# Retention attention and a Mish layer on one core: order of the first two token groups changed

## The chip, the core and the metric

The kernel runs on one core of a Trainium2 chip. A core has five engines that run their own instruction lists and wait for each other by semaphores: TensorE (PE in the profile, with its weight loads as PEld), VectorE (DVE), ScalarE (ACT), GpSimd (POOL) and SyncE (SP). Transfers between the chip's memory and the core's SBUF are issued by GpSimd, SyncE or ScalarE and carried out by 16 DMA engines. TensorE writes only into PSUM, eight banks, from which VectorE and ScalarE read.

The metric is the time of one execution on the device in microseconds (us), as a median of several runs. "Faster" means that this time falls.

## The reference

Two steps follow one another. The first is an attention without softmax, in which an earlier token counts the less the further back it is (factor `lam` per step, one `lam` per head), computed in blocks with a state that is carried on. The second is a layer of two matrix products with Mish between them. The shapes: 4 sequences (batches) of 768 tokens, 8 heads of 64; `w_in` is 512 x 2048, `w_out` 2048 x 512; all inputs and the output are float32.

```python
for b in range(nb):                       # blocks of 64 tokens
    sl = slice(b * block, (b + 1) * block)
    qb, kb, vb = (q[:, :, sl].copy(), k[:, :, sl].copy(), v[:, :, sl].copy())
    intra = np.einsum('bhic,bhjc->bhij', qb, kb) * Dmask[None]
    intra = np.einsum('bhij,bhjd->bhid', intra, vb)
    inter = np.einsum('bhid,bhde->bhie', qb * lam_pow[None], kv_state)
    out[:, :, sl] = intra + inter
    kb_dec = kb * rev_pow[None]
    kv_state = lam_block[None, :, None, None] * kv_state + np.einsum('bhsd,bhse->bhde', kb_dec, vb)
...
h = x @ w_in                              # x: attention output, 3072 tokens x 512
sp = np.where(h > 20.0, h, np.log1p(np.exp(np.minimum(h, 20.0))))
g = h * np.tanh(sp)
return (g @ w_out).astype(np.float32)
```

## The kernel before

The kernel takes blocks of 128 tokens instead of 64. A group n is one such block of all four batches, so 512 tokens; there are six groups, n = 0 to 5. For a group and a batch b the steps are these:

- **Turning k and q.** `turn_pe` transposes k and q of (n, b) on TensorE, four 128 x 128 pieces each, into a PSUM bank (L230), and a copy brings them to SBUF as `kT` and `qT`: by ScalarE (L238), or by VectorE where `by_vector` is set (L236). Later groups use `turn_dma` on SyncE's queue instead.
- **Scores.** `scores` makes eight products of 64 rows into two banks, e and o unless named otherwise (L256), and VectorE multiplies both with the decay mask into `sb` (L260).
- **Outputs.** In group 0 `first_outputs` multiplies `sb` with v so that x comes out transposed (L268), and ScalarE copies it to `xt` (L270). From group 1 on `outputs` adds the part of the state (L276) and of `sb` and v (L281) in one bank, VectorE scales it to `xn` (L284), and the transposition to `xt` is done by DMA or, with `turn` given, by a step `later` on TensorE (L293) and ScalarE (L295).
- **State.** `decay_k` scales k into `kd` (L249, VectorE or GpSimd), `state` multiplies it with v (L302); in group 0 VectorE makes the state `w` from it (L307), later VectorE adds the old state into `raw` (L310) and VectorE or GpSimd scales that to the new `w` (L312).

The first layer works on units of 128 columns of `w_in`. `unit` multiplies one such unit with all 512 tokens (L329) and ScalarE applies Mish (L335); `unit_part` does it for a range of tokens; `two_units` does two units for one half of the tokens (L355, L358). Its banks A, B and C go round. `dense2_plain` is one quarter of the second layer for one batch (L574). From the third group on, parts of both layers are computed with fewer products by sums (`x_sums`, `w_sum`, `token_sum`, `weight_sum`), which the change doesn't touch.

Nothing is scheduled automatically: the order of the calls is the order on each engine's list, and an engine takes its list strictly in that order. Buffers come from named places (`bufs` copies of each), and every PSUM bank is one place, so a step that reuses a bank waits until the last reader of the bank is done. `fill(m)` issues m products of zeros of 128 columns, `busy(m)` such of 512 columns; they keep TensorE busy.

All loads that also convert to 16 bits are issued by GpSimd in one queue (L82, L87, L96, L101). At the start it holds, in order, k and q of batch 1, v of batches 0 and 1, k and q of batches 2 and 3, v of batches 2 and 3, then `win0` in three pieces, `win2`, `win1`, and k, q, v of group 1 with `win3` between them. k and q of batch 0 come by SyncE's and ScalarE's queues.

In group 0 the order is: turn and score batch 0, turn batch 1, outputs of batch 0, scores of batch 1, and so on; `sb` has four places, of which two are used for each batch, so the scores of batch 2 wait for the outputs of batch 0. In group 1 each batch's outputs and state follow soon behind its scores, and the two upper batches are turned with the first lower outputs:

```python
    decay = out1(1)
    turn1(2, "eo")
    decay()
    decay_k(1, 2, nc.vector)
    later[1]()
    turn1(3)
    two_units(1, 0, 0)
    scores(1, 2)
```

Here `out1(b)` issues outputs and state of group 1, and `decay()` is the multiplication of L312 for a lower batch, on VectorE.

Of the kernel before, what the change touches and what calls it, by code (L numbers as in the profile page):

```python
# [8 lines left out]
F16 = mybir.dt.float16  # L9
AF = mybir.ActivationFunctionType  # L10
# [10 lines left out]
def kernel(  # L21
# [98 lines left out]
    load_first("q", 1)  # L120
    load_first("v", 0, 2)
    load_first("k", 2)
    load_first("q", 2)
# [4 lines left out]
    load_first("k", 3)  # L128
    load_first("q", 3)
# [121 lines left out]
    def scores(n, b, tags="eo"):  # L251
# [6 lines left out]
        for t in range(2):  # L258
            sb[n, b, t] = work.tile([128, JP, C], F16, name="sb", tag="sb", bufs=4)
            nc.vector.tensor_tensor(out=sb[n, b, t], in0=p_[t], in1=dm[:, t], op=ALU.mult)  # L260
# [11 lines left out]
    def outputs(n, b, turn=None):  # L272

        po = bank("z", [H, D])
# [361 lines left out]
    turn_pe(0, 1, first_banks, "k")  # L636
    turn_pe(0, 1, first_banks, "q", True)
    head_decays()
    fill(4)
    first_outputs(0, "C")  # L640
    fill(1)
    scores(0, 1, "AB")
    turn_pe(0, 2, first_banks)
    turn_pe(0, 3, first_banks, "k")
    fill(3)
    scores(0, 2)
    turn_pe(0, 3, first_banks, "q")
    first_outputs(1, "C")
    fill(3)
    scores(0, 3, "AB")  # L650
    nc.scalar.preload_act_table(AF.Mish)
    fill(2)
    first_outputs(2, "C")
    fill(4)
    unit_part(0, 0, "G", 0, 2 * C, True)
    first_outputs(3, "z")
    decay_k(0, 0, nc.vector)
    decay_k(0, 1, nc.vector)
    state_decays()
    decay_k(0, 2, nc.vector)  # L660
    decay_k(0, 3, nc.vector)
    unit_part(0, 1, "H", 0, 2 * C, True)
# [6 lines left out]
    unit(0, 3, "B")  # L669

# [10 lines left out]
    turn1 = lambda b, banks="Hz": turn_pe(1, b, banks)  # L681
# [3 lines left out]
    def out1(b):  # L685
        later[b] = outputs(1, b, "G")
        return state(1, b, "H", nc.vector if b < 2 else nc.gpsimd, b < 2)

    state(0, 2, "e", nc.vector)
    state(0, 3, "o", nc.vector)  # L690
# [9 lines left out]
    turn1(0)  # L700
    decay_k(1, 0, nc.vector)
    first_units(7)
# [4 lines left out]
    decay = out1(0)  # L707
    scores(1, 1)
    decay()
    first_units(14)  # L710
    later[0]()
    first_units(15)
    decay = out1(1)
    turn1(2, "eo")
    decay()
    decay_k(1, 2, nc.vector)
    later[1]()
    turn1(3)
# [14 lines left out]
    two_units(1, 10, 0)  # L733
# [5 lines left out]
    later[3]()  # L739
# [343 lines left out]
```

## Time and profile before

| | us |
|---|---|
| median of 3 runs | 206.59 (206.22 to 207.9) |
| profiled execution | 206.84 |
| its span, first to last instruction | 205.1 |
| TensorE busy | 194.9 (95% of the span) |
| VectorE busy | 146.3 (71%) |
| ScalarE busy | 99.8 (49%) |
| GpSimd busy, with its DMA issues | 81.3 (40%) |
| mean granted TensorE clock | 0.99 of full speed |

A row in order of time reads: start, duration, engine, line, operation, output <- input, shape, number, and in brackets how long the engine was idle just before and what ended that. A row of a transfer in the list of issues gives its size and the time from its issue to its landing. Products on TensorE are pipelined: the listed duration overlaps with the next, so the cost of a step is read from where it starts to where the next one starts. A row of a stretch gives its bounds, its length, the busy time of PE, PEld, DVE, ACT and POOL in it, the granted clock, the DMA share and GB/s.

### The profile page before, as it was taken

The page shows a single profiled execution, that of the slowest core. Times are in us where ns is not written, and L with a number is a line of the kernel's source. Part 1 is how long each engine was busy: PE and PEld are TensorE (multiplying, and loading weights), DVE is VectorE, ACT ScalarE, POOL GpSimd, SP SyncE. Part 2 cuts the span into 40 slices and gives each one's busy share as a digit, 9 for nine tenths or more (in the row PEclk, how much of TensorE's full clock was granted, in tenths as well). Part 3 has the DMA queues.
Part 4 walks back from the last instruction along what each step waited for, and adds up shares of the span by engine and source line. Part 5 has one row for each costly group of instructions (what it writes and reads, how often), then busy time and mean ns, then how long its engine had stood idle before and what let it go on. Part 6 is the DMA issues. An engine that isn't in the chain of part 4 may idle for free.

```text
span 205.1 us, 4646 instructions
## 1 busy us (share of the span) xinstructions
PE 194.9 (95%) x1918; PEld 149.9 (73%) x1918; DVE 146.3 (71%) x244; ACT 99.8 (49%) x179; POOL 81.3 (40%) x78
## 2 busy tenths in 40 slices
PE   7699999899999999999998999999999999999990
PEld 3577456688855566667767888888988988888890
DVE  6659628888987977689847698799588667179051
ACT  4566586748431224342263653555474484826300
POOL 7998453551292590848492369230000000000020
PEclk9979999999999999999999999999999999999999
DMA  9999999999989999999999989994112211002133
GB/s 130 139 168 206 174 168 157 173 207 187 122 145 175 202 143 163 166 114 106 140 201 232 120 66 140 187 197 110 29 26 80 76 56 51 0 3 104 50 105 104
DMA packets 109336, 26.26 MB, mean 128 GB/s; under 512 B 99458, under 2 KB 108802, under 8 KB 109314
## 3 DMA queue, kind: packets, MB, share of 16 engines
q0 software_dynamic: 77568, 13.37, 86.0%
q1 hardware_dynamic: 30704, 12.33, 29.2%
q10 hardware_dynamic: 1042, 0.26, 0.6%
q8 instruction: 15, 0.25, 0.5%
q14 instruction: 7, 0.06, 0.1%
HBM read 27.26 MB, written 6.29 MB: 164 GB/s over the span
## 4 chain that ended last, share of the span: by engine, by line
PE 77%; DMA 7%; DVE 6%; ACT 4%; issue 2%; POOL 1%; POOLq 0%; ACTq 0%; DVEq 0%
PE bG L523 13%; PE bH L523 12%; PE bB L412 5%; PE bC L412 4%; PE bA L329 4%; PE bC L329 3%; PE bA L412 3%; DMA xt<-xn 3%; DMA vz<-in_v_dram 3%; PE bB L329 3%; PE bC L355 3%; PE be L256 3%; PE bz L281 2%; PE bB L355 2%; PE bz L276 2%
## 5 line engine op out<-in xcount | busy, mean ns | idle before, releaser
L312 POOL TENSOR_TENSOR w<-raw,lbm 128x512 f16<-128x512 f32 x14 | 20.0, 1431 | 45.0 <-DVE raw L310 45.0
L523 PEld LDWEIGHTS <-gsum 128*128 128x128 f16 x336 | 31.2, 98 | 4.3
L523 PEld LDWEIGHTS <-hsg 128*128 128x128 f16 x240 | 23.0, 98 | 4.4
L605 POOL TENSOR_TENSOR c<-p,u 128x512 f32<-128x512 f32 x1 | 1.3, 1273 | 58.7 <-DVE p L604 58.7
L260 DVE TENSOR_TENSOR sb<-be,dm 128x512 f16<-128x512 f32 x22 | 15.1, 686 | 11.6 <-PE bo L256 10.9
L412 PEld LDWEIGHTS <-wsum 128*128 128x128 f16 x192 | 18.6, 98 | 2.9 <-issue 0.8
L329 PEld LDWEIGHTS <-win 128*128 128x128 f16 x136 | 12.6, 98 | 10.9 <-issue 0.8
L523 PE MATMUL bH<-tsum,gsum 128*128 128x256 f16 x160 | 20.4, 273 | 0.0
L523 PE MATMUL bG<-wout,hsg 128*128 128x256 f16 x160 | 19.9, 273 | 0.0
L284 DVE TENSOR_TENSOR xn<-bz,lq 128x512 f16<-128x512 f32 x20 | 13.7, 686 | 5.5 <-PE bz L281 5.5
L412 PEld LDWEIGHTS <-win 128*128 128x128 f16 x144 | 13.8, 98 | 2.2 <-issue 0.5
L486 DVE TENSOR_TENSOR gsum<-hsg 128x1024 f16<-128x1024 f16 x20 | 15.1, 758 | 0.0
L260 DVE TENSOR_TENSOR sb<-bo,dm 128x512 f16<-128x512 f32 x22 | 14.9, 679 | 0.0
L355 PEld LDWEIGHTS <-win 128*128 128x128 f16 x128 | 12.0, 98 | 2.0 <-issue 0.3
L87 POOL DMA_DIRECT2D kn<-in_k_dram x10 | 11.9, 1194 | 2.8 <-ACT hsg L335 1.5
L87 POOL DMA_DIRECT2D qn<-in_q_dram x10 | 11.7, 1170 | 2.4 <-DMA win<-in_moe_w_in_dram 1.0
L87 POOL DMA_DIRECT2D vn<-in_v_dram x10 | 11.7, 1173 | 1.3 <-DVE w L307 1.0
L412 PE MATMUL bA<-xt,win 128*128 128x256 f16 x80 | 12.0, 272 | 0.1
L416 ACT ACTIVATE hsg<-bC 128x512 f16<-128x512 f32 x10 | 5.9, 594 | 12.4 <-PE bC L412 12.4
L329 PE MATMUL bA<-xt,win 128*128 128x512 f16 x44 | 11.3, 380 | 0.0
L574 PEld LDWEIGHTS <-hsg 128*128 128x128 f16 x64 | 6.0, 98 | 6.9
L335 ACT ACTIVATE hsg<-bA 128x512 f16<-128x512 f32 x11 | 6.6, 599 | 8.1 <-PE bA L329 8.1
(176 smaller groups left out, 444.6 us busy)
## 6 DMA issues: line engine op xcount, KB each, us to landing
out_dram<-osum SPq DMA_DIRECT2D x23, 256.0 KB, 2.5
kn<-in_k_dram POOLq DMA_DIRECT2D x10, 256.0 KB, 9.3
qn<-in_q_dram POOLq DMA_DIRECT2D x10, 256.0 KB, 8.2
vn<-in_v_dram POOLq DMA_DIRECT2D x10, 256.0 KB, 9.9
wout<-in_moe_w_out_dram POOLq DMA_DIRECT2D x4, 512.0 KB, 14.9
win<-in_moe_w_in_dram POOLq DMA_DIRECT2D x3, 512.0 KB, 11.3
vz<-in_v_dram POOLq DMA_DIRECT2D x2, 256.0 KB, 6.3
kn<-in_k_dram POOLq DMA_DIRECT2D x3, 128.0 KB, 5.7
```

What stands on the lines that cost most here:

```text
L87: nc.gpsimd.dma_start(out=tile_, in_=rows(src, n, 2 * bp, 2))
L256: nc.tensor.matmul(p_[t][:, j, :], kT[n, b][rs, j, :], qT[n, b][rs, j, :], start=True, stop=True)
L260: nc.vector.tensor_tensor(out=sb[n, b, t], in0=p_[t], in1=dm[:, t], op=ALU.mult)
L284: nc.vector.tensor_tensor(out=xn, in0=po, in1=bc(lq, 2, D), op=ALU.mult)
L312: decay = lambda: eng.tensor_tensor(out=w_new, in0=raw, in1=lbm, op=ALU.mult)
L329: nc.tensor.matmul(open_[n, ni][:, lo:hi], win[ni // 4][:, kc, (ni % 4) * 128 : (ni % 4) * 128 + 128], xt[n][:, kc, lo:hi], start=(opens a ...
L335: nc.scalar.activation(h_tile(n)[:, ni, :], open_.pop((n, ni)), AF.Mish)
L355: nc.tensor.matmul(t[:, u, :], win[ni // 4][:, kc, m : m + 128], xt[n][:, kc, cs], start=(u == 0 and kc == 0), stop=(kc == NKC - 1), skip_ ...
L412: nc.tensor.matmul(t[:, u, :], lhs, rhs, start=(fresh and u == 0 and kk == 0), stop=(kk == 1), skip_group_check=True)
L486: nc.vector.tensor_tensor(out=gsum[n, i][:, ks, :], in0=a, in1=b, op=op)
L523: nc.tensor.matmul(t, lhs(kk, blk), rhs(kk)[:, lo:hi], start=(fresh and kk == 0), stop=(kk == HK - 1), skip_group_check=True)
L574: nc.tensor.matmul(po, hsg[n][:, ki, b * C : (b + 1) * C], wout[part][:, kk, :], start=(ki == 0), stop=(ki == NKI - 1))
```

## The change

It has three parts, all of them in the order of calls and in places of buffers.

1. Group 0: k and q of all batches are loaded ahead of any v. All four batches are turned and scored first, then all k are scaled, and then the four outputs follow; both copies of each turn are ScalarE's. The products `sb` of the upper two batches get places of their own (those of `xsum`). There are 42 `fill` products in place of 29. Both half units of the first layer come behind all four outputs.
2. Group 1: scores of batch 1 go ahead of the outputs of batch 0; x of both lower batches is turned ahead of the turns of the upper batches, and these stand ahead of the first `two_units`; the outputs and states use other banks; the copies of q go from ScalarE to VectorE; the two `decay` steps of the lower batches go behind the scores of batch 2, the outputs of batches 2 and 3 behind their scores.
3. Group 2: all four quarters of the second layer for batch 0 (`plain2(0, ...)`) go ahead of the scores of batch 2 instead of three.

```diff
     load_first("q", 1)
+    for b in range(2, B):
+        load_first("k", b)
+        load_first("q", b)
     load_first("v", 0, 2)
-    load_first("k", 2)
-    load_first("q", 2)
...
-    load_first("k", 3)
-    load_first("q", 3)
     load_first("v", 2, 2)
...
-            sb[n, b, t] = work.tile([128, JP, C], F16, name="sb", tag="sb", bufs=4)
+            tag, bufs = ("sb", 4) if n > 0 or b < 2 else (f"xsum{b % 2 * 2 + t}", 1)
+            sb[n, b, t] = work.tile([128, JP, C], F16, name="sb", tag=tag, bufs=bufs)
...
-    def outputs(n, b, turn=None):
-
-        po = bank("z", [H, D])
+    def outputs(n, b, turn=None, tag="z"):
+
+        po = bank(tag, [H, D])
...
     scores(0, 0)
-    turn_pe(0, 1, first_banks, "k")
-    turn_pe(0, 1, first_banks, "q", True)
+    turn_pe(0, 1, first_banks)
+    fill(6)
+    turn_pe(0, 2, first_banks)
+    scores(0, 1, "AB")
+    fill(4)
+    turn_pe(0, 3, first_banks)
+    scores(0, 2)
     head_decays()
+    nc.scalar.preload_act_table(AF.Mish)
+    fill(8)
+    scores(0, 3, "AB")
+    for b in range(B):
+        decay_k(0, b, nc.vector)
     fill(4)
     first_outputs(0, "C")
-    fill(1)
-    scores(0, 1, "AB")
-    turn_pe(0, 2, first_banks)
-    turn_pe(0, 3, first_banks, "k")
-    fill(3)
-    scores(0, 2)
-    turn_pe(0, 3, first_banks, "q")
-    first_outputs(1, "C")
-    fill(3)
-    scores(0, 3, "AB")
-    nc.scalar.preload_act_table(AF.Mish)
-    fill(2)
+    first_outputs(1, "e")
+    state_decays()
+    fill(8)
     first_outputs(2, "C")
-    fill(4)
-    unit_part(0, 0, "G", 0, 2 * C, True)
     first_outputs(3, "z")
-    decay_k(0, 0, nc.vector)
-    decay_k(0, 1, nc.vector)
-    state_decays()
-    decay_k(0, 2, nc.vector)
-    decay_k(0, 3, nc.vector)
-    unit_part(0, 1, "H", 0, 2 * C, True)
+    for ni, tag in ((0, "G"), (1, "H")):
+        unit_part(0, ni, tag, 0, 2 * C, True)
...
-    turn1 = lambda b, banks="Hz": turn_pe(1, b, banks)
...
+    def turn1(b, banks, eng=True):
+        turn_pe(1, b, banks, "k")
+        turn_pe(1, b, banks, "q", eng)
+
-    def out1(b):
-        later[b] = outputs(1, b, "G")
-        return state(1, b, "H", nc.vector if b < 2 else nc.gpsimd, b < 2)
+    def out1(b, turn, po, pv):
+        later[b] = outputs(1, b, turn, po)
+        return state(1, b, pv, nc.vector if b < 2 else nc.gpsimd, b < 2)
...
     first_units(9, 10, 11, 4, 5, 6)
-    turn1(0)
     decay_k(1, 0, nc.vector)
+    turn1(0, "Hz")
     first_units(7)
     turn1(1, "GC")
     scores(1, 0)
     decay_k(1, 1, nc.vector)
     first_units(12, 13)
-    decay = out1(0)
     scores(1, 1)
-    decay()
+    decays1 = [out1(0, "G", "z", "H")]
     first_units(14)
+    decays1.append(out1(1, "H", "e", "o"))
     later[0]()
     first_units(15)
-    decay = out1(1)
-    turn1(2, "eo")
-    decay()
-    decay_k(1, 2, nc.vector)
     later[1]()
-    turn1(3)
+    turn1(2, "ze")
+    turn1(3, "oB")
     two_units(1, 0, 0)
     scores(1, 2)
+    for decay in decays1:
+        decay()
+    decay_k(1, 2, nc.vector)
+    two_units(1, 2, 0)
+    two_units(1, 4, 0)
+    scores(1, 3)
+    out1(2, "G", "z", "H")
     decay_k(1, 3, nc.vector)
-    two_units(1, 2, 0)
-    out1(2)
-    scores(1, 3)
-    two_units(1, 4, 0)
     two_units(1, 6, 0)
     later[2]()
-    out1(3)
+    out1(3, "G", "e", "o")
     two_units(1, 8, 0)
+    later[3]()
     two_units(1, 10, 0)
     turn_pe(2, 0, ("H", "z"))
...
-    later[3]()
     two_units(1, 12, 0)
...
-    plain2(0, 0, 1, 2)
+    plain2(0, 0, 1, 2, 3)
     attend(2, 2)
     decay_k(2, 2, nc.vector)
-    plain2(0, 3)
     plain2(1, 0, 1)
```

The loads stand on GpSimd's list. Behind the load of q of batch 1 it read, before (`vz0` is v of batches 0 and 1, `vz1` that of 2 and 3; the two k and two q are those of batches 2 and 3):

```order
L82 DMA vz0_69<-in_v_dram 128x16x64
L82 DMA kn_98<-in_k_dram 128x8x64
L82 DMA qn_100<-in_q_dram 128x8x64
L124 IOTA ek_84 128x1
L126 IOTA eq_85 128x1
L82 DMA kn_98<-in_k_dram 128x8x64
L82 DMA qn_100<-in_q_dram 128x8x64
L82 DMA vz1_70<-in_v_dram 128x16x64
L96 DMA win0_71<-in_moe_w_in_dram 128x4x128 x2
```

And now, at the same place of GpSimd's list:

```order
L82 DMA kn_97<-in_k_dram 128x8x64
L82 DMA qn_99<-in_q_dram 128x8x64
L82 DMA kn_97<-in_k_dram 128x8x64
L82 DMA qn_99<-in_q_dram 128x8x64
L82 DMA vz0_69<-in_v_dram 128x16x64
L125 IOTA ek_84 128x1
L127 IOTA eq_85 128x1
L82 DMA vz1_70<-in_v_dram 128x16x64
L96 DMA win0_71<-in_moe_w_in_dram 128x4x128 x2
```

The first v has moved behind four loads and the two iotas behind it; from the second v on, the list is the same.

On VectorE's list the scores, states and decays of group 1 stand as follows before, from the lower batches' `w` on (`w0`, `w1`: the two decays of lower batches; `kd_648`, `kd_693`: scaled k of batches 2 and 3; `sb` from banks e and o: scores of batch 2, then of batch 3):

```order
L284 TENSOR_TENSOR xn_624<-bz_611,lq_150 128x512
L310 TENSOR_TENSOR raw_631<-bH_626,w1_405 128x512
L312 TENSOR_TENSOR w1_405<-raw_631,lbm_134 128x512
L249 TENSOR_TENSOR kd_648<-kn_119,lk_149 128x512
L260 TENSOR_TENSOR sb_689<-be_679,dm_148 128x512
L260 TENSOR_TENSOR sb_691<-bo_680,dm_148 128x512
L249 TENSOR_TENSOR kd_693<-kn_119,lk_149 128x512
L284 TENSOR_TENSOR xn_718<-bz_705,lq_150 128x512
L310 TENSOR_TENSOR raw_725<-bH_720,w2_424 128x512
L260 TENSOR_TENSOR sb_738<-be_728,dm_148 128x512
L260 TENSOR_TENSOR sb_740<-bo_729,dm_148 128x512
```

And now on VectorE's list, from the copies of the upper q on (`kd_703`, `kd_762`: scaled k of batches 2 and 3):

```order
L235 COPY qT_662<-be_657 128x512
L235 COPY qT_662<-bB_670 128x512
L260 TENSOR_TENSOR sb_697<-be_687,dm_148 128x512
L260 TENSOR_TENSOR sb_699<-bo_688,dm_148 128x512
L312 TENSOR_TENSOR w0_410<-raw_602,lbm_134 128x512
L312 TENSOR_TENSOR w1_417<-raw_630,lbm_134 128x512
L248 TENSOR_TENSOR kd_703<-kn_119,lk_149 128x512
L260 TENSOR_TENSOR sb_735<-be_725,dm_148 128x512
L260 TENSOR_TENSOR sb_737<-bo_726,dm_148 128x512
L284 TENSOR_TENSOR xn_752<-bz_739,lq_150 128x512
L310 TENSOR_TENSOR raw_759<-bH_754,w2_436 128x512
L248 TENSOR_TENSOR kd_762<-kn_119,lk_149 128x512
```

Both `w` and the first `kd` have moved from ahead of the first pair of `sb` to behind it, the second `kd` from behind that pair to behind `raw`, and the second pair of `sb` ahead of the `xn` and `raw` of batch 2.

More of the change, by code (lines that the diff above doesn't have):

```diff
@@ L669 @@
     unit(0, 3, "B")
+    state(0, 2, "e", nc.vector)
+    state(0, 3, "o", nc.vector)
     def first_units(*units):
@@ L679, in sums @@
             token_sum(n, i, part)
-    turn1 = lambda b, banks="Hz": turn_pe(1, b, banks)
     ring[0] = 1
     later = {}
-    def out1(b):
-        later[b] = outputs(1, b, "G")
-        return state(1, b, "H", nc.vector if b < 2 else nc.gpsimd, b < 2)
-    state(0, 2, "e", nc.vector)
-    state(0, 3, "o", nc.vector)
+    def turn1(b, banks, eng=True):
[4 more added lines that the diff above has]
+        return state(1, b, pv, nc.vector if b < 2 else nc.gpsimd, b < 2)
     first_units(8)
```

## The prediction

> **What bounds the kernel now.** I read the summary of engines first, then the busy time by stretches, then the order of time through the first 60 us, then the software queue's landings. The summary names TensorE:
>
> ```profile
> PE 194.9 (95%) x1918; PEld 149.9 (73%) x1918; DVE 146.3 (71%) x244; ACT 99.8 (49%) x179; POOL 81.3 (40%) x78
> ```
>
> A mean over the span says nothing about the two stretches that are edited. Their rows (PE, PEld, DVE, ACT, POOL busy us, then granted clock) say more:
>
> ```profile
> 0.00:19.28 19.28, 15.57 (x157) 11.24 (x158) 13.05 (x31) 12.13 (x22) 17.43 (x25) 0.91 1.65 158
> 19.28:46.52 27.24, 26.37 (x265) 17.45 (x266) 19.54 (x32) 17.40 (x32) 14.48 (x14) 1.00 1.98 178
> ```
>
> Up to 19.28 us TensorE is idle for 3.7 us, and the stretch ends in a load. From 19.28 to 46.52 it is idle for only 0.87 us, with VectorE busy for 72%. So the first stretch can gain only by what ends it, and the second is close to TensorE's own work. The rows in order of time that mark the first stretch's end:
>
> ```profile
> 9.76 1.03 PE L268 MATMUL bC<-sb,vz 128*128 128x128 f16 x8 [1.42 <-DMA vz<-in_v_dram]
> ...
> 19.28 1.41 PEld L329 LDWEIGHTS <-win 128*128 128x128 f16 x8 [0.21 <-DMA win<-in_moe_w_in_dram]
> ...
> 20.82 0.68 DVE L307 TENSOR_TENSOR w<-bo,lbm 128x512 f16<-128x512 f32 x1
> ...
> 21.02 0.39 PE L302 MATMUL be<-vz,kd 128*128 128x128 f16 x4
> ...
> 21.55 0.38 PE L302 MATMUL bo<-vz,kd 128*128 128x128 f16 x4
> ...
> 21.77 1.03 PE L329 MATMUL bC<-xt,win 128*128 128x512 f16 x4
> ...
> 22.64 1.03 PE L329 MATMUL bA<-xt,win 128*128 128x512 f16 x4
> ```
>
> The wait for v at 9.76 (1.42 us) is what the first edit is about. But the unit (0,2) starts at 19.28 because the third piece of `win0` lands then, ten microseconds later. After that, state (0,3) starts at 21.55 and not at 21.24 (21.02 and one state, 0.22): its bank o is read by `w<-bo` until 21.50. Then units follow each 0.87 us.
>
> **Part 1: loads and first group.** The queue's order is changed only among k, q and v of the first group; the bytes ahead of the second v and of every `win` piece are the same. Issue time plus time to landing gives when they arrive:
>
> ```profile
> 8.33 1.17 POOL L82 DMA_DIRECT2D vz<-in_v_dram  x1
> vz<-in_v_dram POOLq DMA_DIRECT2D x1, 256.0 KB, 6.4
> 10.94 1.54 POOL L96 DMA_DIRECT2D win<-in_moe_w_in_dram  x2
> win<-in_moe_w_in_dram POOLq DMA_DIRECT2D x1, 512.0 KB, 9.5
> 15.41 0.86 POOL L96 DMA_DIRECT2D win<-in_moe_w_in_dram  x1
> win<-in_moe_w_in_dram POOLq DMA_DIRECT2D x1, 512.0 KB, 14.2
> ```
>
> The second v lands at 8.33 + 6.4 = 14.7, `win2` at about 11.7 + 9.5 = 21.2 (it is the second issue of its row), `win3` at 15.41 + 14.2 = 29.6. I keep these for the new kernel. With all scores ahead, what is left behind 14.7 is two outputs, four half units and two states: 2 x 0.46 + 4 x 0.44 (half of a unit's 0.87) + 2 x 0.22 = 3.1 us, so TensorE is through at about 17.9 at the earliest and then waits for the same load at 19.28. The gain there is the 0.21 us or less of before. The 13 added `fill` matmuls (128 columns, 0.055 us each by four in 0.22, below) are 0.7 us ahead of that wait and cost nothing; 1.4 us of spare time hides them and a v that is late by up to as much. Without this cover they would cost their 0.7 us. The two small iotas now issue behind the first v; the three Exp that read them have moved further back still, behind the last turn, and nobody is kept waiting.
>
> What it does gain lies behind: decay_k and the block mask now stand ahead of the outputs on VectorE, so `w` of batches 0 and 1 is done before 20.8 and the wait in front of state (0,3) goes. Unit 8 starts at 21.77 - 0.31 = 21.46, with `win2` there since 21.2. That is term one, **-0.31 us**; between 0 (if the load lands 0.3 later) and -0.57 (21.2 - 21.77: `win2` lets no more).
>
> **Part 2: second group.** In the trace of before, its marks are these:
>
> ```profile
> 30.00 1.04 PE L329 MATMUL bB<-xt,win 128*128 128x512 f16 x4
> ...
> 30.42 0.64 ACT L238 ACTIVATE qT<-bC 128x512 f16<-128x512 f16 x1
> ...
> 31.11 1.02 PE L329 MATMUL bC<-xt,win 128*128 128x512 f16 x4
> ...
> 36.70 0.59 ACT L238 ACTIVATE qT<-bo 128x512 f16<-128x512 f16 x1
> ...
> 37.18 0.60 ACT L295 ACTIVATE xt<-bG 128x512 f16<-128x512 f16 x1
> ...
> 37.83 1.03 PE L355 MATMUL bC<-xt,win 128*128 128x256 f16 x8 [0.18 <-ACT xt L295]
> ...
> 38.80 0.23 PE L256 MATMUL be<-qT,kT 64*128 64x128 f16 x1
> ...
> 39.23 0.69 DVE L260 TENSOR_TENSOR sb<-be,dm 128x512 f16<-128x512 f32 x1 [0.91 <-PE bo L256]
> ...
> 46.52 1.04 PE L355 MATMUL bC<-xt,win 128*128 128x256 f16 x8
> ```
>
> And the prices, from where one piece starts to where the next does:
>
> ```profile
> 35.10 0.68 DVE L312 TENSOR_TENSOR w<-raw,lbm 128x512 f16<-128x512 f32 x1
> ...
> 35.70 0.69 DVE L284 TENSOR_TENSOR xn<-bz,lq 128x512 f16<-128x512 f32 x1
> ...
> 41.11 0.23 PE L256 MATMUL be<-qT,kT 64*128 64x128 f16 x1
> ...
> 41.44 1.05 PE L355 MATMUL bB<-xt,win 128*128 128x256 f16 x8
> ...
> 43.20 0.39 PE L293 MATMUL bG<-ident,xn 128*128 128x128 f16 x4
> 43.42 0.39 PE L276 MATMUL bz<-w,qT 128*128 128x128 f16 x4
> ...
> 43.88 0.39 PE L302 MATMUL bH<-vn,kd 128*128 128x128 f16 x4
> 44.10 1.04 PE L355 MATMUL bA<-xt,win 128*128 128x256 f16 x8
> ...
> 45.85 0.39 PE L230 MATMUL bH<-ident,kn 128*128 128x128 f16 x4
> ```
>
> Scores 0.33; two `two_units` 1.76; one x transposition 0.22; outputs 0.46; a state 0.22; k and q turned, with an x behind, 0.67 (45.85 to 46.52), so 0.44 alone. One VectorE operation behind another: 0.60, its result 0.68 after its start. ScalarE: 0.49.
>
> The walk of the new order: unit 12 comes at 30.00 - 0.31 = 29.69, just behind `win3` (29.6). Unit 13 waited for ScalarE's copy out of bank C, which ends at 31.06; q is now copied by VectorE, idle there, so unit 13 follows at 30.56. Then scores 31.43, outputs(0) 31.76, state 32.22, unit 14 32.44, outputs(1) 33.31, state 33.77, x(0) 33.99, unit 15 34.21, x(1) 35.08, both upper turns 35.30 to 36.18. ScalarE ends the second x near 36.4 (by my estimate Mish of unit 15 from 35.3, x behind it at 0.49 and 0.60 long), so the first `two_units` runs 36.4 to 37.3, and scores (1,2) follow at about 37.4, when ScalarE's second k copy frees bank o. Before it was 38.80: TensorE is 1.4 us ahead here.
>
> VectorE takes it back. Its first product on these scores starts 0.43 behind them (39.23 - 38.80), at S = 37.8. From S its queue holds, in order: two sb, two w, kd(2), two sb, xn(2), raw(2), kd(3). In before both w and a kd were done ahead of the scores; now they stand between the two pairs of sb, while VectorE idles about 1 us ahead of S. kd(2) is the 5th: ready at 37.8 + 4 x 0.60 + 0.68 = 40.9. xn(2) is the 8th: 42.7. kd(3) is the 10th: 43.9. TensorE, from 37.4: scores 37.7, two `two_units` 39.5, scores 39.8, outputs 40.3; state(2) waits for kd(2), **0.6**, until 40.9, ends 41.1; one `two_units` 42.0; x(2) waits for xn(2), **0.7**, ends 42.9; outputs(3) 43.4; state(3) waits for kd(3), **0.5**, ends 44.1; `two_units` 45.0, x(3) 45.2, `two_units` 46.1, turn 46.5. The next `two_units` (12) starts at 46.5; before 46.52. So term two gives back what term one and the turns won: **the sum at this point is 0.0 us**. It hangs on S and ten VectorE operations: per 0.1 us of S 0.1 us; unknown is S by 0.3 either way, and the copies of q on VectorE (0.4 to 0.6 each, four of them; the last two end near 36.9, an idle stretch hides them, else 0.5 each).
>
> **Part 3: third group's scores one part later.** Scores (2,2) and what hangs on them move by one part of the plain layer, 0.87 us, TensorE's work is the same:
>
> ```profile
> 62.25 0.68 DVE L249 TENSOR_TENSOR kd<-kn,lk 128x512 f16<-128x512 f16 x1
> ...
> 64.00 0.39 PE L302 MATMUL bH<-vn,kd 128*128 128x128 f16 x4
> ```
>
> kd ends at 62.93 + 0.87 = 63.80, its reader comes at 64.00: hidden by 0.2 us, cost 0, at worst 0.2 to 0.5. SP's transposition of that x leaves when it did.
>
> **Sum.** The profiled execution took 206.84 (span 205.1 and 1.7 around it); with 0.0 it stays 206.8. It lies 0.25 above the median 206.59, so the forecast is **206.6**. Its own range is 205.9 to 207.3: S, part 3 and the spread of the runs (206.22 to 207.9 before).
>
> **Rivals.**
>
> A, faster: VectorE does not hold up TensorE. Without the three waits (0.6 + 0.7 + 0.5) TensorE's own work brings `two_units` (12) to 44.7, 1.8 us earlier: 204.8; with half of them 205.7. For it: VectorE idles 1 us ahead of S, and all that TensorE needs is 1.8 us. Against it: the queue is in order and its 0.60 is even over many rows. 17%.
>
> B, slower: the half clock falls into the first layer. These stretches show how the clock went down:
>
> ```profile
> 6.20:9.60 3.40, 1.79 (x30) 1.43 (x27) 2.33 (x6) 2.47 (x7) 3.40 (x7) 1.00 2.16 138
> 9.60:13.05 3.45, 3.03 (x30) 2.47 (x30) 1.29 (x2) 1.63 (x3) 3.45 (x5) 0.52 2.40 156
> ```
>
> After 3.4 us in which TensorE was idle for 1.6 us, the next 3.45 us ran at 0.52. In before they lay where loads set the pace. The new kernel idles up to 1.4 us in one piece before 19.28; if that is enough, 19.9 to 23.3 runs at half, where units stand back to back: 1.7 us lost, 208.3. It decides if TensorE's busy time in one such window falls to near 1.8 us. Against it: dense units fill the rest of that window, some 2 us. 12%. [...]
>
> C, slower: GpSimd gets in ahead of kd(3). The rows:
>
> ```profile
> 45.45 1.65 POOL L312 TENSOR_TENSOR w<-raw,lbm 128x512 f16<-128x512 f32 x1 [1.76 <-DVE raw L310]
> ...
> 45.88 1.76 DVE L249 TENSOR_TENSOR kd<-kn,lk 128x512 f16<-128x512 f16 x1
> ```
>
> A kd that starts beside GpSimd's w took 1.76, 1.08 longer. In the new order kd(3) stands right behind raw(2), which releases such a w on GpSimd: if that starts first, state(3) comes 1.1 us later, 207.7. Against it: by the prices kd starts 0.60 behind the start of raw, and w has to wait for raw's result, 0.68 behind it, so kd is first. 7%. [...]
>
> **How the numbers follow.** Forecast 64%, A 17%, B 12%, C 7%. The range 205.0 to 208.0 holds the forecast and C, most of A and little of B. A change under 1% (2.1 us) is about what a measurement of this kernel can't tell from none. Faster by more (under 204.5): A with a first stretch that gains too, 5%. Slower by more (over 208.7): B with a second wait, 6%. Same: 89%.
>
> **What would show it.** In the new trace: TensorE waits for `win` at 19.28 with 1 us or more idle ahead of it; unit 8 near 21.5; scores (1,2) near 37.4; then waits of TensorE for kd, xn, kd of 0.5 to 0.7 each; `two_units` (12) near 46.5. The forecast is wrong if these waits are absent (A), if the granted clock drops behind 19 us (B), or if loads land at other times than before.

## The result, and the profile after

The changed kernel took 205.46 us (median, 205.19 to 206.36); before, run beside it, 207.45 (206.22 to 207.9; 206.5 to 206.7 in the later sets). The ratio is **0.993, interval 0.9906 to 0.9954**: a gain of 1.0 to 1.9 us where none was forecast, inside the stated range and under 1%. The nine times of before lie in two heaps, four from 206.2 to 206.7 and five from 207.4 to 207.9, so its median stands high. The profiled execution of the changed kernel took 206.36, the slowest of its nine, with a span of 204.6.

Its summary of engines has TensorE a little less busy than before (194.9), with 13 matmuls and 13 weight loads more:

```profile
PE 193.8 (95%) x1931; PEld 149.1 (73%) x1931; DVE 147.5 (72%) x247; ACT 98.5 (48%) x176; POOL 81.7 (40%) x78
```

In order of time, the first group of the changed kernel (start, duration, engine, line, operation, then the wait in brackets; the scores are now line 255, `first_outputs` 268):

```profile
13.65 0.62 PE L268 MATMUL bC<-sb,vz 128*128 128x128 f16 x8 [0.95 <-DMA vz<-in_v_dram]
...
15.36 0.62 PE L268 MATMUL bC<-sb,vz 128*128 128x128 f16 x8 [0.19 <-DMA vz<-in_v_dram]
...
16.80 1.21 PEld L329 LDWEIGHTS <-win 128*128 128x128 f16 x12 [0.22 <-DMA win<-in_moe_w_in_dram]
...
18.57 1.03 PE L329 MATMUL bA<-xt,win 128*128 128x512 f16 x4
...
20.74 1.03 PE L329 MATMUL bC<-xt,win 128*128 128x512 f16 x4
```

Unit (0,2) starts at 18.57 with no wait for `win0`, and unit 8 at 20.74 with none for `win2`: 1.03 us ahead of before. The second group:

```profile
31.01 0.23 PE L255 MATMUL be<-qT,kT 64*128 64x128 f16 x1
...
32.62 0.39 PE L281 MATMUL bz<-vn,sb 128*128 128x64 f16 x8 [0.89 <-DMA vn<-in_v_dram]
...
38.01 0.23 PE L255 MATMUL be<-qT,kT 64*128 64x128 f16 x1
...
38.44 0.69 DVE L260 TENSOR_TENSOR sb<-be,dm 128x512 f16<-128x512 f32 x1 [0.90 <-PE bo L255]
...
41.58 0.40 PE L302 MATMUL bH<-vn,kd 128*128 128x128 f16 x4 [0.44 <-DVE kd L248]
...
43.38 0.40 PE L293 MATMUL bG<-ident,xn 128*128 128x128 f16 x4 [0.53 <-DVE xn L284]
...
43.84 0.68 DVE L248 TENSOR_TENSOR kd<-kn,lk 128x512 f16<-128x512 f16 x1
...
44.01 1.64 POOL L312 TENSOR_TENSOR w<-raw,lbm 128x512 f16<-128x512 f32 x1 [1.21 <-DVE raw L310]
...
44.58 0.40 PE L302 MATMUL bo<-vn,kd 128*128 128x128 f16 x4 [0.34 <-DVE kd L248]
...
47.23 1.04 PE L355 MATMUL bC<-xt,win 128*128 128x256 f16 x8
```

The three waits for VectorE are there, in the forecast order. But a wait of 0.89 us for v of the second group has come in ahead of them, and `two_units` (12) starts at 47.23, 0.71 us *later* than before. That lag is the same at every block of scores up to 107 us, except the one that part 3 moved. So in this execution all of the gain, and more, comes behind 107 us, where nothing was edited. Before, there, in order of time:

```profile
101.93 1.19 SPq L287 DMA_TRANSPOSE xt<-xn  x1
...
106.98 0.23 PE L256 MATMUL be<-qT,kT 64*128 64x128 f16 x1
...
108.62 0.43 DVE L390 TENSOR_TENSOR xsum<-xt 128x512 f16<-128x512 f16 x1 [3.85 <-DMA xt<-xn]
...
109.10 0.60 PE L412 MATMUL bC<-xsum,wsum 128*128 128x256 f16 x4 [0.29 <-DVE xsum L390]
...
111.43 0.38 PE L281 MATMUL bz<-vn,sb 128*128 128x64 f16 x7 [0.15 <-DVE sb L260]
...
112.03 0.60 PE L412 MATMUL bB<-xsum,wsum 128*128 128x256 f16 x4 [0.22 <-DVE bC L437]
```

And the changed kernel:

```profile
102.64 1.19 SPq L287 DMA_TRANSPOSE xt<-xn  x1
...
107.69 0.23 PE L255 MATMUL be<-qT,kT 64*128 64x128 f16 x1
...
107.91 0.42 DVE L390 TENSOR_TENSOR xsum<-xt 128x512 f16<-128x512 f16 x1 [2.42 <-DMA xt<-xn]
```

Both have the same work here. The first row is the issue of a transpose of x, and the row of L390 the first operation of VectorE that reads it. From the issue of the last transpose of x in the fourth group, the `x_sums` start 6.7 us later in before (101.93 to 108.62) and 5.3 us later after the change. VectorE's late start then makes TensorE wait three times. The stretches between two blocks of scores, by engine (length, busy us of PE, PEld, DVE, ACT, POOL, granted clock, DMA share, GB/s), before:

```profile
106.98:113.44 6.46, 5.79 (x62) 4.60 (x62) 4.75 (x10) 2.92 (x6) 2.00 (x2) 1.00 1.81 216
```

and after:

```profile
107.69:112.96 5.27, 5.27 (x61) 4.53 (x61) 4.97 (x10) 2.81 (x6) 2.00 (x2) 1.00 1.60 179
```

1.19 us less, TensorE idle for 0.67 of them before and not at all after; the other 0.52 is listed as busy. Why a transpose 50 us behind the last big edit lands sooner was the question for the chip.

### The profile page after: what moved, and what is told of

Its sections match the earlier page's. It is cut to its first block, busy times and chain, and to the rows that moved or that the text cites. A ratio compares the mean times of both kernels' runs of the same rounds, so it can differ in the third digit from the quotient of the medians.

```text
span 204.6 us, 4668 instructions
## 1 busy us (share of the span) xinstructions
PE 193.8 (95%) x1931; PEld 149.1 (73%) x1931; DVE 147.5 (72%) x247; ACT 98.5 (48%) x176; POOL 81.7 (40%) x78
## 4 chain that ended last, share of the span: by engine, by line
PE 76%; DMA 9%; POOL 7%; DVE 3%; ACT 2%; issue 1%; POOLq 0%; DVEq 0%; ACTq 0%
PE bG L523 15%; PE bH L523 13%; DMA vn<-in_v_dram 8%; PE bB L412 6%; PE bC L412 5%; PE bA L412 4%; PE bA L329 3%; PE bB L329 3%; PE be L255 2%; PE bC L355 2%; POOL win L96 2%; PE bC L329 2%; PE bz L281 2%; PE bA L574 2%; PE bA L355 2%; PE bB L355 2%
## 5 line engine op out<-in xcount | busy, mean ns | idle before, releaser
L284 DVE TENSOR_TENSOR xn<-bz,lq 128x512 f16<-128x512 f32 x18 | 12.3, 686 | 3.7 <-PE bz L281 3.7
## 6 DMA issues: line engine op xcount, KB each, us to landing
wout<-in_moe_w_out_dram POOLq DMA_DIRECT2D x4, 512.0 KB, 15.4
```

Source lines behind the costliest of these rows:

```text
L284: nc.vector.tensor_tensor(out=xn, in0=po, in1=bc(lq, 2, D), op=ALU.mult)
```

## The experiments

**Which part?** Four kernels: before again, the first part alone (loads, first group and the places of its scores), the second group alone, and the changed kernel with VectorE's queue set in another order. The last edit:

```diff
+    for decay in decays1:
+        decay()
+    decay_k(1, 2, nc.vector)
     two_units(1, 0, 0)
     scores(1, 2)
-    for decay in decays1:
-        decay()
-    decay_k(1, 2, nc.vector)
     two_units(1, 2, 0)
```

> The kernel before, unchanged, timed against itself, with a new profile. Its nine times lie in two heaps, 206.2 to 206.7 and 207.4 to 207.9. If the heaps come from the half clock of TensorE falling at different places, the runs with the lower mean granted clock (0.990) are in the slower heap and the new profile shows the half clock at another place than 9.6 to 13.05 us. If they come from the loads, the clock is the same in both heaps and landings differ. Ratio to itself 1.000, within 0.004 either way.

> Loads and first group changed, the rest as before. First-group theory: this part alone has the whole gain, ratio 0.993, about 1.5 us less, and the second group passes on the 1.0 us by which the new trace is ahead at 21 us. The forecast's theory: at most 0.3 us less (ratio 0.9985), as the first layer waits for its weights. Second-group theory: ratio 1.000.

> Second group changed, loads and first group as before, third group as before. Second-group theory: ratio 0.993, about 1.5 us less. First-group theory: ratio 1.000. VectorE theory (of the forecast): TensorE is ahead by about 1 us at the scores of batch 2 and has lost that again by the twelfth two_units, with three waits of 0.3 to 0.7 us for kd, xn and kd; ratio 1.000 or up to 1.003.

> The new kernel with both lower decays and the scaling of k of batch 2 moved ahead of the first two_units on VectorE's list, where it idles about 1 us. VectorE theory: state of batch 2 no longer waits, the twelfth two_units comes about 0.6 us earlier than in the new kernel, and the time falls by 0.6 us against it, ratio to before about 0.990. If the loads and transpositions of the fourth group set the time (TensorE's lead is lost in waits near 108 us), the mark comes earlier but the time stays at ratio 0.993. If the three waits cost nothing, no mark moves.

Measured ratios: before_again 0.9984 (0.9958 to 1.0009), part1_only **0.9902** (0.9871 to 0.9933), part2_only **1.0023** (0.9997 to 1.0048), early_decays 0.9906 (0.9872 to 0.9939). The gain is in the first part; the second adds about 0.5 us, not told apart from nothing by its interval. Its profile has the same three waits at the same prices, in order of time:

```profile
42.20 0.40 PE L302 MATMUL bH<-vn,kd 128*128 128x128 f16 x4 [0.44 <-DVE kd L249]
...
43.99 0.40 PE L293 MATMUL bG<-ident,xn 128*128 128x128 f16 x4 [0.53 <-DVE xn L284]
...
45.19 0.40 PE L302 MATMUL bo<-vn,kd 128*128 128x128 f16 x4 [0.34 <-DVE kd L249]
```

In early_decays the first of these waits is gone, the second is 0.29 and the third stays; its time is not told apart from the changed kernel's. The wait for v at 32.6 is not always there: part1_only has it (0.83), early_decays has not, and by GpSimd's waits that v landed anywhere from 30.1 to 32.9 us in these profiles.

Up to here all profiles of kernels with the first part, and none without it, had the late gain. Two causes seemed able to reach that far: the addresses in SBUF, since the `xsum` and `kd` tiles are now set aside ahead of `xt`, or the order itself.

**Addresses or order?** before_moved is before with the first part's addresses; part1_pinned is the first part with before's. order_only is the first part with the loads in before's order.

```diff
 # before_moved: decay_k and scores keep a place that is already set aside
 ...
 # before_moved: behind scores(0, 0)
+    for i in range(4):
+        sb[0, 2 + i // 2, i % 2] = work.tile([128, JP, C], F16, name="sb", tag=f"xsum{i}", bufs=1)
+    for b in range(B):
+        kd[0, b] = work.tile([128, H, D], F16, name="kd", tag="kd", bufs=4)
 # part1_pinned: in scores, for n == 0 and b >= 2
+                sb[n, b, t] = wsum[3][:, 2 * (b - 2) + t].rearrange("p a (c d) -> p (a c) d", d=C)
 # part1_pinned: behind scores(0, 0)
+    x_tile(0)
```

> The order of before on every engine, and in SBUF the addresses that the first part alone gives: the scores of the two upper batches of group 0 in the xsum tiles, and the kd tiles set aside ahead of xt, so that xt, kd, hsg, xn and all that stand behind them start 4 to 8 KB elsewhere in each partition. Place theory (the addresses make the loads and the transposes by DMA of the later groups land sooner): the first two groups as before, scores(1,2) 8.8 to 9.2 us behind scores(1,0) as before, and between 107 and 113 us the gain of 1.0 to 1.2 us that the three kernels with the first part have; the transpose of x issued near 102 lands in 5.2 us rather than 6.7; ratio 0.994 to 0.995. Order theory (what is early in the first group stays early up to the fourth): no gain anywhere, ratio 0.998 to 1.001.

> The first part alone in its own order, with every tile at its address of before: the scores of the two upper batches of group 0 lie in wsum3, which nothing writes before the third stage, and xt is set aside ahead of kd. Place theory: the first group ahead as in the first part alone (unit 8 and scores(1,0) 1.0 to 1.6 us earlier than before), about 0.6 us left of it from 48 to 107 us because of the wait for v, and no further gain between 107 and 113; ratio 0.996 to 0.998. Order theory: as the first part alone, 0.990 with 1.0 to 1.2 us of the gain between 107 and 113.

> The first part's order of work with the loads issued in the order of before (v of the lower batches ahead of the last two k and q), and the first part's addresses. If the loads carry the gain of the first group: the turns of batches 2 and 3 wait 0.5 to 1.2 us more for k and q, v is never waited for, and unit 8 starts within 0.3 us of before's; the time lies 0.8 to 1.2 us above the first part alone, ratio 0.994 to 0.996. If the order of work alone carries it (outputs behind all scores, the decays before them): the ratio of the first part alone, 0.990 within 0.002.

before_moved 0.9995 (0.9968 to 1.0022), part1_pinned 0.9911 (0.9879 to 0.9943): the place theory falls on both. order_only was a miss: 0.9992 (0.9962 to 1.0021) where 0.994 to 0.996 was expected. Yet its profile has the late gain. It loses that in the first group, where TensorE waits for k as expected, and longer; the granted clock then is 0.5 from 12.5 to 16.0 us (0.990 in the mean of this execution), and eleven of its twelve runs have a mean clock of 0.980 to 0.990:

```profile
10.04 0.40 PE L230 MATMUL bG<-ident,kn 128*128 128x128 f16 x4 [1.74 <-DMA kn<-in_k_dram]
```

So the late gain hangs on neither the loads' order nor the addresses. One thing was left that all kernels with it share: the 13 more `fill` products, which with their weight loads are 26 more TensorE instructions.

**The count of instructions.** The page of before lists a DMA queue that no line of the kernel issues (transfers, MB, share of 16 engines):

```profile
q8 instruction: 15, 0.25, 0.5%
```

15 transfers of 16 KB, against 3,836 TensorE instructions (1,918 matmuls and as many weight loads): 256 for each on average (3,836 / 15). That they are the fetches of TensorE's instructions is an estimate from these counts, which the next runs put to the test. The stretch of DMA in which one shows says when it came. The edits change this count and hardly the work: products on zeros are cut finer or joined.

```diff
 # before_finer and part1_finer (+26)
-    busy(3)
+    fill(13)
     lamb = bank("C", [H])
     nc.tensor.matmul(lamb, one1, lam1, start=True, stop=True)
-    busy(3)
+    busy(2)
+    fill(4)
 # part1_coarser (-26 against the first part), both places, and one fill less
-    fill(8)
+    busy(2)
 # loads_only: the diff of the loads alone, on before
```

> Before with 26 more TensorE instructions in the first 4.6 us, of the same work: three 512-column products on zeros become 13 and one becomes 4, all of 128 columns; nothing else moves. What is tested is the queue that brings TensorE's instructions (q8, one transfer of 16 KB for 256 instructions, 15 in all). In every kernel without the first part it fetches 0.4 to 1.1 us after the transpose of x that is issued near 95.5 us (96 in before); in every kernel with it, which has 26 more TensorE instructions, 1.3 to 2.3 us ahead of that transpose (93 in the first part alone). Fetch theory: the late gain of 1.0 to 1.2 us hangs on that alone, so this kernel has it between 107 and 113 us, VectorE waits 2.4 to 2.8 us rather than 3.8 for x near 106 to 108, and the ratio is 0.994 to 0.996 with the first two groups as in before. Rival, that the order of the first group brings it in another way: no gain at 107 to 113, ratio 0.998 to 1.001.

> The first part alone with 26 fewer TensorE instructions for the same work on zeros: twice 8 products of 128 columns become 2 of 512, and one product is left out. Fetch theory: the first group as in the first part alone (scores(1,0) near 28.1), the fetch behind the transpose near 95 us again, no gain between 107 and 113, ratio 0.995 to 0.997. Rival: 0.990 to 0.991 as the first part alone.

> The first part alone with 26 more TensorE instructions in the first 4.6 us as above, so that each fetch comes another 1.5 to 2 us earlier. Fetch theory: the fetch near 93 moves to 91 to 92, still ahead of the transpose of x near 95 but close to the issue of v's load at 91; the gain at 107 to 113 stays between half and the whole of 1.1 us, and other fetches meet other transfers, which can give or take up to 1 us anywhere behind 48 us; ratio 0.986 to 0.996. Rival: 0.990 to 0.991, every mark behind 48 us as in the first part alone.

> Before with only the order of the loads changed: v of the lower batches behind all k and q. The order of work is before's, so the first outputs, which stand ahead of scores(0,1) on TensorE, wait for v until it lands near 13 us rather than 9.7, and three more blocks of scores and two turns stand behind that wait: scores(1,0) 2 to 3.3 us later than in before, less what is given back at the wait for the last third of win0 at 19.3 (up to 1.4), so 1 to 2.5 us later at scores(1,2) and the ratio 1.004 to 1.012. If the loads alone carry the gain of the first group: ratio 0.994 to 0.997.

before_finer: **0.9946** (0.9922 to 0.997), from a kernel that differs from before only in its first 5 us, in how zeros are multiplied. From the second group up to 106.67 its blocks of scores start within 0.03 us of those of before_again; then, in order of time:

```profile
101.62 1.19 SPq L288 DMA_TRANSPOSE xt<-xn  x1
...
106.90 0.42 DVE L391 TENSOR_TENSOR xsum<-xt 128x512 f16<-128x512 f16 x1 [2.43 <-DMA xt<-xn]
```

part1_coarser: 0.9975 (0.9951 to 0.9999), with the late gain gone:

```profile
107.70 0.42 DVE L390 TENSOR_TENSOR xsum<-xt 128x512 f16<-128x512 f16 x1 [3.93 <-DMA xt<-xn]
```

part1_finer: 0.9896 (0.9869 to 0.9924). loads_only was a miss in size: 1.0161 (1.0128 to 1.0194), worse than the 1.004 to 1.012 expected. TensorE waits 5.44 us for v, and then runs at half clock as well; the wait, and the busy time of the stretch behind it with the granted clock (third from the right):

```profile
13.51 1.04 PE L267 MATMUL bC<-sb,vz 128*128 128x128 f16 x8 [5.44 <-DMA vz<-in_v_dram]
```

```profile
13.05:16.50 3.45, 2.73 (x27) 2.18 (x28) 1.27 (x2) 1.33 (x3) 3.45 (x5) 0.50 1.77 183
```

**Which fetch, and is it by steps?** In the changed kernel, with 25 instructions more, all 15 fetches come 0.4 to 3.8 us earlier than in before (the first at 15.4 for 17.2, the last at 194.0 for 196.2). So the count was also changed only between the fetches at 82 and 96 us (units of the first layer cut in two columns of 256, at nearly equal TensorE time: in before eight products of 256 columns cost 0.88 us, four of 512 cost 0.87), only behind the latter, and at the start by half.

```diff
 # in unit, for n == 2: the units 5, 6, 7 (split_ahead), 12, 13, 14 (split_behind), 4 to 9 (split_more), counted from 0 in the order of calls
+    for kc in range(NKC):
+        for lo in (0, HC):
+            nc.tensor.matmul(
+                open_[n, ni][:, lo : lo + HC],
+                win[ni // 4][:, kc, (ni % 4) * 128 : (ni % 4) * 128 + 128],
+                xt[n][:, kc, lo : lo + HC], start=(kc == 0 and lo == 0),
+                stop=(kc == NKC - 1), skip_group_check=True)
 # before_half_finer
-    busy(3)
+    busy(1)
+    fill(8)
     lamb = bank("C", [H])
```

after_coarser is the changed kernel with the edits of part1_coarser, early_finer is early_decays with those of before_finer.

> Before with the twelve 512-column products of three units of the first layer (those at 85.3, 86.2 and 88.6 us) each cut in two of 256 columns: the same work, 24 more TensorE instructions, all between the fetches of instructions at 82 and at 96. The fetches up to 82 stay; the one at 96 comes 1.3 to 2 us earlier, ahead of the transpose of x at 95.3. If that fetch is the cause: the marks up to 107 as before within 0.3 us (what the cut itself costs), a gain of 1.0 to 1.2 us between 107 and 113, VectorE's wait for x near 2.4 rather than 3.8, ratio 0.994 to 0.997. If one of the earlier fetches is: no gain, ratio 0.999 to 1.002.

> The same cut in the three units at 98.8, 101.2 and 103.0 us, all behind the fetch at 96 and ahead of that at 112. If the fetch at 96 is the cause: it stays, so no gain between 107 and 113, VectorE waits 3.8 us for x, ratio 0.999 to 1.002. If the cut itself helps or hurts, it shows here: a step of more than 0.3 us at the marks from 97.6 to 107.

> The whole change with 26 fewer TensorE instructions for the same work on zeros (twice 8 products of 128 columns become 2 of 512, and one is left out), so TensorE has one instruction less than before. Fetch theory: what the forecast summed is then all there is: the first group ahead by 0.5 to 1.0 us, the three waits for VectorE as in the changed kernel, no gain between 107 and 113, ratio 0.997 to 1.000. Rival, that the change has another gain that the count of instructions only adds to: 0.994 or less.

> Before with 12 more TensorE instructions in the first 2.6 us (two products of 512 columns become 8 of 128), so that the fetch near 96 comes 0.6 to 1.2 us earlier and falls beside the issue of the transpose at 95.3. If the fetch has only to come ahead of that transpose, the result is one of the two known ones: ratio 0.9995 with 3.8 us of waiting for x, or 0.9945 with 2.4. If it goes by degrees: 0.996 to 0.998 and a wait of 2.8 to 3.4.

> Before with the 512-column products of six units of the first layer (83.1 to 91.6 us) each cut in two of 256 columns: 48 more TensorE instructions, all between the fetches at 82 and 96, so that the latter comes near 91 to 92.5. If that fetch alone carries the gain: marks up to 107 as before, 1.0 to 1.2 us between 107 and 113 in the profile, ratio 0.994 to 0.996, as before_finer. If the earlier fetches have a share: 0.996 to 0.999, as split_ahead.

> The changed kernel with both decays and the third k decay ahead of the third group of scores (as early_decays), and 26 more TensorE instructions in the first 4.6 us. If the pieces add up: the second group ends 0.5 to 1.5 us earlier than in the changed kernel and each fetch comes 1.5 to 2 us earlier still: ratio 0.987 to 0.990. If the first part alone is all there is: 0.990 to 0.992, as early_decays.

In one table, worked out from the profiles: TensorE instructions against before (kernels with the second group's edit have one semaphore instruction less), the start of the 0.2 us in which the fetch shows, the issue of the transpose of x near 95.5 us, how far the fetch is behind it, VectorE's wait for x near 107, and the time between the two blocks of scores above:

| kernel | instructions | fetch | transpose | fetch behind it by | wait for x | between scores | ratio |
|---|---|---|---|---|---|---|---|
| before | 0 | 96.6 | 95.60 | +1.0 | 3.85 | 6.46 | 1 |
| before_again | 0 | 96.6 | 95.30 | +1.3 | 3.87 | 6.49 | 0.9984 |
| before_moved | 0 | 96.0 | 95.27 | +0.7 | 3.79 | 6.41 | 0.9995 |
| part2_only | -1 | 98.3 | 96.92 | +1.4 | 4.08 | 6.69 | 1.0023 |
| part1_coarser | 0 | 95.8 | 94.59 | +1.2 | 3.93 | 6.55 | 0.9975 |
| after_coarser | -1 | 96.2 | 96.17 | +0.0 | 3.46 | 6.09 | 1.0009 |
| loads_only | 0 | 100.3 | 99.39 | +0.9 | 3.90 | 6.51 | 1.0161 |
| split_behind | +24, behind | 95.0 | 95.28 | -0.3 | 3.84 | 6.44 | 1.0011 |
| before_half_finer | +12 | 93.6 | 95.30 | -1.7 | 2.54 | 5.27 | 0.9948 |
| split_ahead | +24, between | 93.2 | 95.31 | -2.1 | 2.58 | 5.28 | 0.998 |
| split_more | +48, between | 93.0 | 96.49 | -3.5 | 1.53 | 5.28 | 0.9934 |
| before_finer | +26 | 92.8 | 95.28 | -2.5 | 2.43 | 5.27 | 0.9946 |
| order_only | +26 | 94.0 | 96.18 | -2.2 | 2.42 | 5.27 | 0.9992 |
| part1_only | +26 | 93.2 | 94.97 | -1.8 | 2.44 | 5.28 | 0.9902 |
| part1_pinned | +26 | 91.8 | 94.08 | -2.3 | 2.57 | 5.28 | 0.9911 |
| after | +25 | 94.0 | 96.30 | -2.3 | 2.42 | 5.27 | 0.993 |
| early_decays | +25 | 92.6 | 94.13 | -1.5 | 2.82 | 5.43 | 0.9906 |
| early_finer | +51 | 91.6 | 95.41 | -3.8 | 2.74 | 5.36 | 0.9901 |
| part1_finer | +52 | 91.2 | 94.88 | -3.7 | 1.95 | 5.28 | 0.9896 |

Wherever the fetch falls from 0.3 us ahead of that transpose to 1.4 behind it, the stretch takes 6.1 to 6.7 us; wherever it comes 1.5 to 3.8 us ahead, 5.3 to 5.4. With 12 instructions the whole gain is there (0.9948, 0.9923 to 0.9973). But the fetch came 3.0 us earlier (93.6 for 96.6), where 0.6 to 1.2 was expected; why 12 instructions move it so far was not settled, and no run placed it between 0.3 and 1.5 us ahead of the transpose. So there are two levels and nothing seen between; how sharp the step is was not tested. split_more (0.9908 to 0.9959) has the gain with all fetches up to 82 us in their places, so what changes from the one near 96 on is enough; split_behind (0.9987 to 1.0035), with the same kind of cut elsewhere, has nothing. Its next fetch, at 109.3 us, is as early as that of split_more, so the gain is not that one's. split_ahead is half a miss: its profiled execution has the whole step, its timed runs (205.16 to 207.47; interval 0.9955 to 1.0005) only part of it; five of its twelve have a clock of 0.986 to 0.992, and the median of the other seven is 205.82, against 206.44 for the runs of before with 0.993 or more. early_finer (0.9873 to 0.9929) shows no sum of the helpful pieces beyond the first part.

after_coarser (0.9984 to 1.0034) is the changed kernel without the change of count: **no change, as was forecast**. The fastest kernels are the first part alone and its finer form, near 0.99, with early_decays and early_finer not told apart from them.

What the fetch does in between can be seen in part. Landing times of what was issued from 86 to 100 us (median us, last column), before:

```profile
vn<-in_v_dram POOLq DMA_DIRECT2D x2, 256.0 KB, 9.9
...
xt<-xn SPq DMA_TRANSPOSE x2, 5.0
kT<-kn SPq DMA_TRANSPOSE x1, 3.1
```

and before_finer:

```profile
vn<-in_v_dram POOLq DMA_DIRECT2D x2, 256.0 KB, 8.1
...
xt<-xn SPq DMA_TRANSPOSE x2, 4.4
kT<-kn SPq DMA_TRANSPOSE x1, 4.9
```

With the fetch early, one transpose of k lands 1.8 us later and nobody is late for it; the loads and transposes of x behind it land earlier.

The traces of before_again and before_finer, whose marks agree up to here, show part of how. Soon behind the fetch DMA moves little for more than a microsecond, 7 GB/s in the one and 24 in the other. In before_again this is from 97.0 to 98.25 us (last column: GB/s), behind the issue of the transpose of x at 95.30:

```profile
93.50:95.00 1.50, 1.50 (x23) 1.23 (x22) 1.12 (x4) 0.60 (x1) 1.49 (x2) 1.00 0.62 44
97.00:98.25 1.25, 1.25 (x16) 0.79 (x15) 1.22 (x2) 0.60 (x1) 1.25 (x2) 1.00 0.26 7
```

In before_finer DMA is at its slowest ahead of that transpose, in a stretch in which before_again moved little too:

```profile
93.50:95.00 1.50, 1.50 (x23) 1.23 (x22) 1.12 (x4) 0.60 (x1) 1.49 (x2) 1.00 2.67 24
97.00:98.25 1.25, 1.25 (x16) 0.80 (x15) 1.22 (x2) 0.60 (x1) 1.25 (x2) 1.00 1.83 156
```

The other kernels divide in the same way: within 4 us behind the issue of that transpose, the lowest rate over 1 us is 4 to 13 GB/s in the eight profiles of the upper level (6.1 to 6.7 us between scores) and 58 to 148 GB/s in the eleven of the lower. That the fetch makes the pause is argued from this, as the pause moves with it; why 16 KB can do it was not settled.

## Why the prediction was right or wrong

- **The step that failed** is the one that priced the filler: "The 13 added `fill` matmuls … are 0.7 us ahead of that wait and cost nothing." Their time on TensorE was indeed covered. But they are 26 instructions, which move the later fetches of instructions, and this was worth 1.1 us by before_finer (0.0054 of 206.6; 1.0 by the medians of runs with a clock of 0.993 or more, 206.49 and 205.53) and 1.6 by after_coarser against the changed kernel (1.0009 to 0.993; by their medians 206.78 and 205.46, with no clock below 0.993 in either, 1.3). The sum stopped at 46.5 us and took everything behind it as shifted only; from 47 to 107 us that held to 0.02 us, and then it did not.
- **Landings kept as in before**: wrong, by its own mark. TensorE was to wait for `win0` at 19.28 with a microsecond idle; it found it landed at 18.57. Unit 8 came at 20.74 rather than 21.46. Term one (-0.31, at most -0.57) was mis-sized in the profile, -1.03. Part of that is lost again at v (0.89 in this execution); timed, the first part without its added instructions is worth 0.5 us (part1_coarser, 0 to 1.0).
- **The first group needs both halves of its edit**: the loads alone cost 3.3 us (1.0161), the order alone, with the late gain in its profile, brought nothing (0.9992), together they gain. The forecast did not take them apart.
- **VectorE gives back what the turns win**: right. The waits were 0.44, 0.53 and 0.34 for 0.6, 0.7 and 0.5, with S at 38.4 for 37.8. The second group alone measured +0.5 us where the forecast had +0.3 (its 0.0 less term one).
- **Part 3** at no cost: right as far as it shows. In the changed kernel the moved scores start 0.86 us later against their neighbours, and the next mark has the old lag again.
- **Rival A**, VectorE not holding TensorE up, did not happen; its time (204.8 to 205.7) was met in another way, which is luck. **Rival B**: the granted clock was 1.00 through the first layer. And the 0.52 of before at 9.60 to 13.05 us cost little: before_again ran the same stretch at full clock (third from the right), and its scores (1,0) start 0.29 us earlier (29.38 for 29.67).

```profile
9.60:13.05 3.45, 2.53 (x42) 1.77 (x42) 1.29 (x2) 2.26 (x4) 3.45 (x5) 1.00 2.36 151
```

In split_more the half clock fell later, and cost more:

```profile
11.90:15.30 3.40, 3.32 (x34) 2.66 (x32) 1.60 (x3) 1.80 (x4) 3.40 (x4) 0.50 1.98 174
```

Its scores (1,0) start at 30.51; those of split_ahead and split_behind, with the same order up to there and at full clock in that stretch, at 29.36: 1.15 us, against 0.29 in before. The forecast asked only whether the change would bring the half clock in. It overlooked that before pays for it in some runs: of the 122 timed beside the later kernels (one of 1109.77 us left aside), 44 have a mean clock below 0.993, and so have all that took more than 206.8. The change may take it out: all 66 runs of the eight kernels with the first part and its loads have 0.993 or more. So have the twelve of before_finer, and no run separates this from the rest of the first part.

- **Rival C**: GpSimd's w started at 44.01, behind kd at 43.84, and kd took 0.68.
- **Sum**: -0.5 for the first part, +0.5 for the second and -1.1 to -1.6 for the fetch give -1.1 to -1.6; measured -1.45. The 1.6 is taken from that same measurement, so only the 1.1 checks it. The first two are what was forecast as 0. The -0.5 may in part be the clock, and the -1.45 also holds the five runs of before near 207.7, whose clocks are not known: against before's later runs with a clock of 0.993 or more (medians 206.44 to 206.63), the changed kernel's median is 1.0 to 1.2 us less.

## What to carry to other kernels

An edit that adds or removes TensorE instructions, filler included, can move later fetches of instructions: near 96 us one came at 92.8 for 96.6 with 26 more (before_finer), and at 95.8 for 93.2 with 26 fewer (part1_coarser against part1_only). Beside loads and transposes that are waited for, such a fetch was worth a microsecond here (6.46 us against 5.27 between two blocks of scores), 50 us behind the edit: compare the fetches of the two traces before a gain is put down to the edit's own work. Time a control that changes the count of instructions and no work, as cutting a product on zeros finer does. And when two orders are changed together (loads and the work that reads them), each alone can lose what both gain. Compare the granted clocks of the runs, too, before a median is compared.

## What the runs showed of the hardware

A DMA queue of instructions, q8, brought 15 transfers of 16 KB against 3,836 TensorE instructions, 256 for each on average. That it is TensorE's is an estimate; it fits that 26 more of them in the first 5 us brought the transfer near 96 us 3.8 us earlier (before_finer, 92.8 for 96.6). Each took 0.9 to 1.9 us of one DMA engine in the stretches read (27.5 to 58% of 16 engines for 0.2 us). TensorE itself did not stop at the one read for this: in the changed kernel's 107.69 to 112.96 us, with a fetch at 108.8, it is busy for all of the 5.27 us. For loads beside a fetch it was otherwise: those of v issued from 86 to 100 us landed after 9.9 us in before and 8.1 in before_finer (medians), and the place of one fetch decided 1.2 us (6.46 against 5.27), at two levels with none seen between, and 12 instructions were enough to go from one to the other (before_half_finer, 0.9948). Behind the fetch near 96 us DMA moved 7 GB/s for 1.25 us (before_again), against 156 in the same stretch of before_finer, whose fetch is at 92.8. Moving `xt`, `kd` and the tiles behind them to other addresses in SBUF changed nothing that could be measured (before_moved, 0.9995).
